# PSUM reads that may run on either of two engines, and a new table for the order of the work: complex-decay linear attention with a token-mixing stage, fp32, one core

## The chip, the cores and the metric

The kernel runs on one core of a Trainium2 chip. The metric is the device time of one execution in microseconds (us). The profile comes from one execution, recorded by the hardware profiler.

## The reference

Two stages follow each other. The first is a linear attention with a complex decay: for each batch (4) and head (8) a 48x48 complex state is decayed and updated in each of 768 steps. The second gates the result by a phase, mixes it over tokens, and adds a channel product:

```python
mag = np.sqrt(a_re * a_re + a_im * a_im)
scale = np.minimum(mag, 0.999) / (mag + 1e-06)
a_re_n, a_im_n = (a_re * scale, a_im * scale)
for t in range(S):
    new_re = ar * S_re - ai * S_im
    new_im = ar * S_im + ai * S_re
    kv = np.einsum('bhd,bhe->bhde', k[:, :, t], v[:, :, t])
    S_re, S_im = (new_re + kv, new_im)
    y[:, :, t] = np.einsum('bhd,bhde->bhe', q[:, :, t], S_re)
...
theta = x @ w_theta                       # x: y as [batch, token, 384]
zr = x * np.cos(theta)
zi = x * np.sin(theta)
y = np.einsum('ts,bsd->btd', w_tok_r, zr) + np.einsum('ts,bsd->btd', w_tok_i, zi)
u = x + y
return (u + np.maximum(u @ w_ch, 0.0)).astype(np.float32)
```

The attention's inputs are fp32. The four weights are float64.

## The kernel before, in words

**Tiling.** The 768 tokens of a batch are cut into six chunks of 128, so there are 24 chunks `n`, each a tile of 128 tokens by 384 = 8 heads x 48. For each chunk `front_a` (L596) takes logarithms of the decay, and TensorE sums them along the tokens with a triangular matrix (`tric`); `front_p` (L674) does the same for the phase (`triq`; the last row of the chunk before comes in through `sel`), rounds it to whole turns by adding a large constant (into `cssn`), and takes sine and cosine. `back` (L713) multiplies `k` and `q` by decay and phase (tiles `hw`), turns them (`kT`, `qT`), forms the masked scores, the chunk's output `x` and the next state. The first four chunks do this in fp32 with TensorE transposes (`old`); later ones split each value into two fp16 halves and turn them by DMA. `theta` (L946) forms the phase of the second stage and `z`, the sine and cosine parts of `x`; `moe_part` and `moe` (L982, L991) mix them over the tokens with `w_tok_r` and `w_tok_i` and add the channel product. The weights arrive as float64, are put together from their bits by three VectorE instructions into a PSUM bank, and are then split into two fp16 halves (`w_load`, `w_split`; the first half is made by `scaled`, L530).

**What sets the order.** The functions above don't issue anything. Each call is recorded as an operation of a `Plan` (L273 on), with the engines that it may run on; `either` (L290) records one that has a form for each of several engines. `order` (L350) then reads a table, `PLACES` (L119), which holds for each step the number of an operation and which of its engines runs it. A negative number stands for a filler, a matmul of constants whose result nobody reads; it goes into a PSUM buffer that is free at that step and is left out where none is free. `emit` (L381) issues the work in the order of the table, so each engine runs its operations in that order. In the profile every operation has line L396, a filler L388, a load of ScalarE's function table L392.

```python
if place < 0:
    kind = next((x for x in PSUM if room.get(x)), None)
...
op = self.ops[place >> 2]
op.engine, op.load = op.engines[place & 3], None
```

**Buffers.** SBUF is divided into pools of equal buffers by size: A (384 fp32 a partition, 48 of them), B (768), C and H for turned tiles, D for scores, E and V for small ones. PSUM has four banks (`bank`; one is kept for scores) and two double banks (`pair`). The names in the rows are these pools, not the variables.

**What may run where, before.** Reading PSUM, `scaled` and `absolute` (L540) use ScalarE only. So do the rounding of the phase in `front_p` and in `theta`, the copies of `kT` and `qT` in the first four chunks, the eviction of `x`, that of `acc` in `moe_part`, and the final Relu in `moe`. Other operations had a choice before: many products between ScalarE, VectorE and POOL.

Of the kernel before, what the change touches and what calls it, by code (L numbers as in the profile page):

```python
# [29 lines left out]
SV = 1.0  # L30
# [101 lines left out]
|RaI3}QQO=Gzaeah8`6fn;ok^s1UEt(KU4*_BRYI1w!PXQcE}xO+qxayuB+H>YA3uA*@$k$HsTwJjU=4hNWrO%G@OC6a6{Ep<#cUTOZ7Ybk5qO{zpXY_)Zc@@vq$elb>SThD
Pqy%9Gr&>a1oBfzfzarGF*YHa1E}*4Y&!n;5OWWyKoOqZ}i~-%<d%Mh??6O!u(EhJGGtO&TMD5bKCjt!gg`Hv|Zk=Y)93<R{ur!8?~?#Q;*=7PTmoB{5u_0V5g_AZfA4}U0n
BPIIW&<FSeK4t8D-VVF-p{1g>qPFb3mrMx9mn^#gr<yRqHeZf&=>JKNpu-gbX`usz%!ZI8EuI|Mw`7Y{-^C1VK~>Hk9qZufLKbxYmUIk3FCpw8<i+tclWuBdCPnN4={FE9zu
wkeo~xlIO+s~hU%&g5jQXJHPO(3CErE*$VMzbU{XEWtADhXZgB4#8nK0t=hsrnD(<{%>7J9fi9p|7Kt_xLMNGHtU;>&Cq6eGqM@ojBUm@o13l8_GV(Uulo;p2A6dceP^?~+1
u=IcGX$kKktHjZCyq8jc%Z;>XMt8-JveK+f#{qgU#XQXcO9l_h$O3zH~6&oNVTH^Sg!J>1J`av|HY->{fScyY=11ZgaP<9;jQpL-j~KR!`LJ-Olc8v%5Q0&(yu$xq80Y-yQ4
@cNglVdbGPzGkbG*0WaYdJl+M=pc+z7c40N51`m_EKC;kDd&nNThwlNJUmV!?7Mq|ZvJ>5j?VxH&BWu7dXv?n&Xo8xMCai(CBATcsrip73n(1zQ2UDkYfBPG}o!I$b2e{g>7
srwsLQSbjbxNZ%I`(F}kOtNu8hH=dLN%BM*PvV27QRJjNDZZ-HH?PUa2j4CXhaRMmD)+~WOlMUX-!6x)#NmJO+i!Clr&{cMN`$(G<8iw)6}#yZ4J3aZP8oI7Q4l5rMEI${Fb
nl-O6o=Ti<B9y8KpQtGHF#8tG_t31ig$)7Y`JRo<#>&2)3!LbuedbigjS3+-07YFqFwvRmJ3Y&EygU2K=wt7EyH)>eC~v(?qG>Ym2GH`fRDcud|}>8B?GCSv$5yUXqJyTY!x
EA7g={@uVXju1$2H?-T=3^YScc$Y-FTh)VKU=lXcj5QO@R5R1m4k*OA_e+e}{l`7jNFzNpW{m9C52Cw`g9b+KQoC~vz02&zcH_H=-Q;fkc%i|KiR08RVO(k=`_cW_etf@)CH  # L140
9m1sr~eRW<R^1+t2SS_P)Je*e~vv_RIT~{m_1OzqViBUunP{U`N=)^s58XC}WNN=6-9xy&v9Zkpz~+I{O^b-EUz$@+&N|7u}2P#rG0>$-UHGdM~q=-}$fI>|So~ci0b)e~&>
sDNH~LJNdohPHCsSBb>F&ZLE0!9EwO`ud-9!sqKvR>O14T#?EAKx;NXK?=^Q?JBz*Lo*zqN@D8#wK!(T&Y43D)x;wp{)gG`9?*Bpc*WLfz?e9SQgPi~t#EN_Wy(=Ly;zt5V5
D6h+B!Wbd7!pSkND@gQX(WSWk>L)!Kic{B-VB)|3uKH;kQ_2QSt2W>v{&A%>{a(_d-c7>UULuG&m*bh^s#>D&pUrTY3;T5I(yx{-d=xius7TTwCFyzkMDz8NDFHbEvm(|xR%
# [313 lines left out]
def fast_path(ctx, tc, gst, q, k, v, a_re, a_im, w_theta, w_tok_r, w_tok_i, w_ch, out):  # L457
# [72 lines left out]
    def scaled(o, i, m, n=DM):  # L530
# [834 lines left out]
```

## Time and profile before

| | before |
|---|---|
| time, median of 3 runs | 415.62 us (413.92 to 416.1) |
| the profiled execution | 416.11 us |
| its span, first to last instruction | 414.4 us |
| mean granted TensorE clock | 0.987 |
| busy: TensorE, VectorE, ScalarE, POOL | 379.7, 366.3, 366.3, 237.6 us |
| fillers | 2 |

The engines are PE (TensorE), PEld (its weight loads), DVE (VectorE), ACT (ScalarE), POOL (GpSimd) and SP (which issues most DMAs). A row of a timeline gives the start, the time of the group, engine, line, operation, output <- inputs, their sizes, how many instructions (x2), and in brackets the engine's idle time just before and what ended it. Drawn times of successive instructions overlap; the distance between two starts tells how fast they follow each other.

### The profile page before, as it was taken

The page shows a single profiled execution, that of the slowest core. Times are in us where ns is not written, and L with a number is a line of the kernel's source. Part 1 is how long each engine was busy: PE and PEld are TensorE (multiplying, and loading weights), DVE is VectorE, ACT ScalarE, POOL GpSimd, SP SyncE. Part 2 cuts the span into 40 slices and gives each one's busy share as a digit, 9 for nine tenths or more (in the row PEclk, how much of TensorE's full clock was granted, in tenths as well). Part 3 has the DMA queues.
Part 4 walks back from the last instruction along what each step waited for, and adds up shares of the span by engine and source line. Part 5 has one row for each costly group of instructions (what it writes and reads, how often), then busy time and mean ns, then how long its engine had stood idle before and what let it go on. Part 6 is the DMA issues. An engine that isn't in the chain of part 4 may idle for free. (4 is left out here: it accounts for less than half of the span.)

```text
span 414.4 us, 9851 instructions
## 1 busy us (share of the span) xinstructions
PE 379.7 (92%) x3431; PEld 262.7 (63%) x3431; DVE 366.3 (88%) x820; ACT 366.3 (88%) x784; POOL 237.6 (57%) x282
## 2 busy tenths in 40 slices
PE   0789999989999999999899999988999999999994
PEld 0268786656676667777566676665667766566662
DVE  5977799989999999999999989899999998785675
ACT  6988999989999898999899999998889895685985
POOL 1054854496789889587646565686677778210000
PEclk9999999699999999999999999999999999999998
DMA  7888882686979898898975899969999999999994
GB/s 231 292 276 289 286 269 89 213 219 168 183 163 206 128 213 191 189 176 206 232 156 107 177 228 174 223 167 216 215 234 183 176 176 257 224 316 354 306 346 157
DMA packets 162934, 89.23 MB, mean 215 GB/s; under 512 B 119360, under 2 KB 161344, under 8 KB 162880
## 3 DMA queue, kind: packets, MB, share of 16 engines
q1 hardware_dynamic: 162880, 88.55, 87.4%
q8 instruction: 28, 0.46, 0.4%
q14 instruction: 26, 0.21, 0.2%
HBM read 55.05 MB, written 4.72 MB: 144 GB/s over the span
## 5 line engine op out<-in xcount | busy, mean ns | idle before, releaser
L396 PE MATMUL bank<-B,B 128*128 128x384 f16 x864 | 170.8, 326 | 0.1
L396 POOL TENSOR_TENSOR A<-A,A 128x384 f16<-128x384 f32 (+2 forms) x86 | 86.6, 1017 | 45.9 <-DMA A<-in_k_dram 21.6
L396 PEld LDWEIGHTS <-B 128*128 128x128 f16 x864 | 79.6, 98 | 47.3 <-issue 6.0
L396 PEld LDWEIGHTS <-C 96*128 96x128 f16 x888 | 64.2, 102 | 20.2 <-issue 5.3
L396 PE MATMUL bank<-C,C 96*128 96x128 f16 (+1 forms) x544 | 59.0, 231 | 5.9 <-ACT D L396 2.0
L396 PE MATMUL bank<-A,D 128*128 128x48 f32 (+1 forms) x448 | 58.6, 232 | 1.2 <-issue 0.7
L396 POOL TENSOR_SCALAR A<-A 128x384 f16<-128x384 f32 (+1 forms) x64 | 41.1, 643 | 32.3 <-ACT A L396 10.5
L392 ACT ACT_TABLE_LOAD x45 | 57.7, 1283 | 0.7
L396 PEld LDWEIGHTS <-A 128*128 128x128 f16 x432 | 39.4, 98 | 25.0 <-DMA A<-A 4.2
L396 ACT ACTIVATE A<-A 128x384 f32<-128x384 f32 (+2 forms) x106 | 52.7, 516 | 2.6 <-DMA A<-in_a_re_dram 2.4
L396 PE MATMUL pair<-A,A 128*128 128x384 f16 x216 | 49.5, 325 | 2.5 <-DMA A<-A 1.1
L396 PE MATMUL bank<-A,C 96*128 96x48 f16 (+1 forms) x456 | 47.3, 194 | 0.0
L396 ACT ACTIVATE B<-B 128x384 f32<-128x384 f32 (+1 forms) x81 | 45.4, 573 | 1.4 <-DMA B<-in_a_re_dram 0.7
L396 DVE SCALAR_TENSOR_TENSOR A<-bank,A 128x384 f32<-128x384 f32 (+1 forms) x69 | 37.6, 551 | 9.6 <-PE bank L396 6.2
L396 PE MATMUL bank<-A,A 128*128 128x384 f16 x216 | 44.3, 325 | 0.7 <-DMA A<-A 0.5
L396 ACT ACTIVATE A<-bank 128x384 f32<-128x384 f32 (+1 forms) x81 | 37.3, 487 | 6.7 <-PE bank L396 5.4
L396 PEld LDWEIGHTS bank<-A,D 128*128 128x128 f32 x256 | 38.6, 190 | 4.2 <-POOL D L396 1.0
L396 POOL TENSOR_TENSOR B<-A,B 128x768 f32<-128x768 f32 x18 | 33.0, 1833 | 9.8 <-ACT B L396 6.6
L396 POOL TENSOR_SCALAR_AFFINE_SELECT D<-D 128x512 f32<-128x512 f32 x32 | 22.6, 706 | 27.7 <-ACT D L396 22.1
L396 ACT ACTIVATE pair<-pair 128x384 f32<-128x384 f32 x72 | 34.6, 480 | 2.7 <-DVE pair L396 1.8
L396 DVE SCALAR_TENSOR_TENSOR A<-A,A 128x384 f32<-128x384 f32 (+2 forms) x59 | 35.5, 610 | 0.3 <-ACT A L396 0.2
L396 DVE SCALAR_TENSOR_TENSOR bank<-B,bank 128x384 int32<-128x384 int32 x60 | 33.1, 558 | 1.2
(142 smaller groups left out, 751.9 us busy)
## 6 DMA issues: line engine op xcount, KB each, us to landing
B<-in_moe_w_tok_r_dram SPq DMA_DIRECT2D x24, 384.0 KB
B<-in_moe_w_tok_i_dram SPq DMA_DIRECT2D x24, 384.0 KB
A<-in_a_re_dram SPq DMA_DIRECT2D x24, 192.0 KB
A<-in_a_im_dram SPq DMA_DIRECT2D x24, 192.0 KB
A<-in_v_dram SPq DMA_DIRECT2D x24, 192.0 KB
A<-in_k_dram SPq DMA_DIRECT2D x24, 192.0 KB
A<-in_q_dram SPq DMA_DIRECT2D x24, 192.0 KB
out_dram<-A SPq DMA_DIRECT2D x24, 192.0 KB
```

The source lines that it names most:

```text
L392: nc.scalar.preload_act_table_set(op.load)
L396: getattr(getattr(nc, op.engine), name)(*[val(x) for x in op.a], **{k: val(x) for k, x in kw.items()})
```

## The change

Seven places get a second engine: `scaled` and `absolute` on PSUM, the two roundings, the `kT`/`qT` copies, `acc`, `x` and the final Relu may each run on ScalarE or on VectorE. A new helper `moved` records such a copy. Computation and matmuls are the same. The table `PLACES` is another one: it sets the order, the engines and the fillers, of which 14 are built instead of 2 (the table has 15 marks; at one no buffer is free). In all 113 operations run on another engine than before. Of the new freedom the table uses, from ScalarE to VectorE, five Relus, four roundings `pn`, three roundings `cssn`, five weight scalings, one `kT` and one `qT` copy, six splittings (`shl`, `z`) and one absolute value; no `x` and no `acc` moves. The other moves are among engines that were allowed before. One output store is issued by POOL instead of SP.

```diff
 PLACES = """
-c-jrt;cLQ<f$;Iz#x}OmMjPAM#x}OGjcsgW8{62%8r#^$Hn#4;dvM^u0|y>BaNxj!0}mW{;DG}N4jede4-OnS@W6o&_`)AJaNxj!0}tGT0}p(_f%o8n$DaKO-&fyH2#5f|H3
...
+c-k#@VQ2!4f#sNt$(W30G-EO*V;qw)8Iv&?lQ9{SF&UFF8Iv)whkLkS!37I0*u#Pa3l=O`u;79P3ocl&U=IrxEV$r;3;wWR!37HzEVy6~3of`|!985?_^urH{=WC%{d$iF03
...
         if i.root.kind in PSUM:
-            ways = (("scalar", "mul", ca(n, True), ways[0][3]),)
-            return pl.either(*ways)
+            return pl.either(("scalar", "mul", ca(n, True), ways[0][3]), ways[2][:2] + (cv(n),) + ways[2][3:])
...
         if i.root.kind in PSUM:
-            return ac.activation(out=o, in_=i, func=AF.Abs, c=AP_)
+            return pl.either(("scalar", "activation", AP_, dict(out=o, in_=i, func=AF.Abs)),
+                             ("vector", "tensor_scalar", C1, dict(out=o.bitcast(I32), in0=i.bitcast(I32), scalar1=ABS_BITS,
+                                                                  scalar2=None, op0=ALU.bitwise_and)))
...
+    def moved(o, i, n, m=None, add=None):
+        pl.either(("scalar", "activation", ca(n, True), dict(out=o, in_=i, func=AF.Identity, **({} if m is None else dict(scale=m)),
+                                                             **({} if add is None else dict(bias=add)))),
+                  ("vector", "tensor_scalar", cv(n), dict(out=o, in0=i, scalar1=m or 1.0, scalar2=None, op0=ALU.mult) if add is None
+                   else dict(out=o, in0=i, scalar1=add, scalar2=None, op0=ALU.add)))
...
-        ac.activation(out=cs, in_=v3(ph[:, :DM]), func=AF.Identity, bias=MAGIC * SPH, c=AP_)
+        moved(cs, v3(ph[:, :DM]), DM, add=MAGIC * SPH)
...
-                    ac.copy(out=hT[nm].of(g)[:R, 4 * g:4 * g + 4].rearrange("r h t -> r (h t)"), in_=tp[:R], c=ca(512, True))
+                    moved(hT[nm].of(g)[:R, 4 * g:4 * g + 4].rearrange("r h t -> r (h t)"), tp[:R], 512)
...
-        ac.activation(out=rn, in_=th[:, :DM], func=AF.Identity, bias=MAGIC * SP, c=AP_)
+        moved(rn, th[:, :DM], DM, add=MAGIC * SP)
...
-        ac.activation(out=cp[:, :DM], in_=cp[:, :DM], func=AF.Relu, scale=1.0 / SP, c=AP_)
+        pl.either(("scalar", "activation", AP_, dict(out=cp[:, :DM], in_=cp[:, :DM], func=AF.Relu, scale=1.0 / SP)),
+                  ("vector", "tensor_scalar", C1, dict(out=cp[:, :DM], in0=cp[:, :DM], scalar1=0.0, scalar2=1.0 / SP,
+                                                       op0=ALU.max, op1=ALU.mult)))
```

TensorE at the start of the program, before. `tric` and `triq` are the scans of the first two chunks, `sel` the row carried into the second; the 96x48 matmuls form the first state out of the tile `hw` (B_179), those with `ident` are its transposes.

```order
L396 MATMUL bank_232<-A_127,tric 128x384
L396 MATMUL bank_231<-A_123,tric 128x384
L396 MATMUL bank_232<-A_129,triq 128x384
L396 MATMUL bank_233<-A_131,triq 128x384
L396 MATMUL bank_233<-A_150,sel 128x384
L396 MATMUL bank_232<-A_134,B_179 96x48
L396 MATMUL bank_230<-ident,B_179 96x128 x4
L396 MATMUL bank_232<-A_134,B_179 96x48 x7
```

The same place now, after the four scans; the second piece follows two transposes later:

```order
L397 MATMUL bank_233<-A_153,sel 128x384
L389 LDWEIGHTS tri_108
L389 MATMUL bank_232<-ones,tri_108 128x256
L389 LDWEIGHTS tri_108
L389 MATMUL bank_232<-ones,tri_108 128x256
...
L397 MATMUL bank_230<-ident,B_179 96x128 x2
L389 LDWEIGHTS tri_108
L389 MATMUL bank_233<-ones,tri_108 128x256
L397 MATMUL bank_232<-A_141,B_179 96x48 x5
```

Five fillers stand between `sel` and the first transposes, and two more among the transposes and state matmuls.

VectorE at the start, before, ahead of the product that makes the first `hw` (B_179, the last row). `A<-A,A` with one operation are products and squares for chunks 2 and 3; the rows on `B_17x` put weights together.

```order
L396 SCALAR_TENSOR_TENSOR A_127<-A_127,bank_231 128x384
L396 TENSOR_TENSOR A_132<-A_132,A_130 128x384
L396 SCALAR_TENSOR_TENSOR A_138<-bank_233,A_138 128x384
L396 TENSOR_TENSOR A_130<-A_132 128x384
L396 TENSOR_TENSOR A_133<-A_133,A_137 128x384
L396 TENSOR_SCALAR bank_233<-B_172 128x384
...
L396 TENSOR_TENSOR A_137<-A_133 128x384
L396 SCALAR_TENSOR_TENSOR A_150<-B_176,bank_232 128x384
...
L396 TENSOR_TENSOR B_179<-A_136,B_176 128x768
```

The same now:

```order
L397 SCALAR_TENSOR_TENSOR A_123<-A_123,bank_231 128x384
L397 SCALAR_TENSOR_TENSOR bank_233<-B_171,bank_233 128x384
L397 TENSOR_SCALAR A_138<-bank_233 128x384
L397 SCALAR_TENSOR_TENSOR A_138<-bank_233,A_138 128x384
L397 TENSOR_SCALAR bank_233<-B_173 128x384
...
L397 TENSOR_TENSOR A_132<-A_147,A_132 128x384
L397 SCALAR_TENSOR_TENSOR A_153<-B_178,bank_232 128x384
L397 TENSOR_SCALAR B_178<-A_153 128x8x48
...
L397 TENSOR_TENSOR B_179<-A_132,B_178 128x768
```

The two products and two squares are gone (three to POOL, one square to ScalarE), and `A_138<-bank_233`, the scaling of a block of `w_theta`, has come.

ScalarE in a stretch that the profile shows at 37 to 48 us, before. `C` are turned `q` and `k` tiles, `bank<-A` and `A<-pair` belong to decay and phase, `B<-B` and `B<-A` to the phase.

```order
L396 COPY C_202<-bank_230 96x512
L396 ACTIVATE B_195<-bank_233 128x384
L396 ACTIVATE A_130,g_xsum<-bank_232 128x384
L396 COPY C_200<-bank_230 96x512
L392 ACT_TABLE_LOAD
L396 ACTIVATE B_188<-A_144 128x8x48
L396 ACTIVATE D_210<-bank_230 128x512
L396 ACTIVATE B_188<-B_188 128x8x48
L392 ACT_TABLE_LOAD
L396 ACTIVATE bank_233<-A_166 128x384
L396 ACTIVATE B_196<-bank_231 128x384
L396 COPY C_202<-bank_230 96x512
```

The same now:

```order
L397 ACTIVATE C_202<-bank_230 96x512
L397 ACTIVATE B_192<-bank_231 128x384
L397 ACTIVATE A_139,g_xsum<-bank_232 128x384
L393 ACT_TABLE_LOAD
L397 ACTIVATE B_190<-A_128 128x8x48 x2
L397 ACTIVATE D_210<-bank_230 128x512
L397 ACTIVATE B_190<-B_190 128x8x48
L393 ACT_TABLE_LOAD
L397 ACTIVATE bank_231<-A_170 128x384
L397 ACTIVATE A_153<-A_151 128x384
L397 ACTIVATE A_140<-pair_234 128x384
```

The two copies that followed the first (`C_200` and again `C_202`) have left ScalarE for VectorE, an absolute value (one of the two `B_190<-A_128`) has come, and the copies that stay are ACTIVATE instead of COPY.

## Rows read from the trace of the kernel before

**Rows 1.** The page's busy time: us (share of the span) and instructions.

```profile
PE 379.7 (92%) x3431; PEld 262.7 (63%) x3431; DVE 366.3 (88%) x820; ACT 366.3 (88%) x784; POOL 237.6 (57%) x282
```

**Rows 2.** Windows by stage: us, then PE, PEld, DVE, ACT, POOL, PEclk, DMA, GB/s.

```profile
0.00:24.00 24.00, 10.40 (x28) 5.67 (x28) 18.78 (x46) 19.42 (x37) 2.06 (x20) 1.00 0.83 270
24.00:40.00 16.00, 14.62 (x77) 11.70 (x77) 11.32 (x22) 13.05 (x29) 10.25 (x10) 1.00 0.80 271
40.00:100.00 60.00, 56.27 (x412) 41.62 (x411) 54.98 (x122) 57.68 (x120) 38.42 (x44) 0.94 0.71 212
100.00:340.00 240.00, 230.93 (x2324) 160.34 (x2323) 228.12 (x489) 222.68 (x461) 173.18 (x192) 1.00 0.90 188
```

**Rows 3.** The chain that ended last, its longest piece: start us, us, what.

```profile
378.71 25.18 PE bank L396 x160
```

**Rows 4.** Timeline of TensorE, 12 to 46 us.

```profile
12.64 2.93 PE L396 MATMUL bank<-A,tric 128*128 128x384 f32 x4 [12.64 <-DMA B<-in_moe_w_tok_r_dram]
...
21.10 0.55 PE L396 MATMUL bank<-A,B 128*96 128x48 f32 x2 [0.55 <-DVE B L396]
...
26.19 2.08 PE L396 MATMUL bank<-C,C 96*128 96x128 f32 x8 [0.50 <-ACT E L396]
28.06 1.49 PE L396 MATMUL bank<-A,tric 128*128 128x384 f32 x2
...
33.23 1.91 PE L396 MATMUL bank<-C,C 96*128 96x128 f32 x8
...
39.16 1.10 PE L396 MATMUL bank<-C,C 96*128 96x128 f32 x8
...
45.24 0.81 PE L396 MATMUL bank<-A,tric 128*128 128x384 f32 x2
```

**Rows 5.** Timeline of VectorE at 16 to 17 us.

```profile
16.56 0.55 DVE L396 TENSOR_SCALAR bank<-B 128x384 int32<-128x384 int32 x1
17.02 0.55 DVE L396 SCALAR_TENSOR_TENSOR A<-bank,A 128x384 f16<-128x384 f32 x1
```

**Rows 6.** Timeline of POOL, its first instruction of the work.

```profile
24.25 1.95 POOL L396 TENSOR_TENSOR A<-A,A 128x384 f32<-128x384 f32 x2 [21.55 <-DMA A<-in_k_dram]
```

**Rows 7.** Timeline of ScalarE, 20 to 36 us.

```profile
20.59 0.49 ACT L396 ACTIVATE B<-bank 128x384 f32<-128x384 f32 x1 [0.54 <-PE bank L396]
20.98 0.48 ACT L396 ACTIVATE A<-bank 128x384 f16<-128x384 f32 x1
...
28.30 0.60 ACT L396 ACTIVATE D<-bank 128x512 f32<-128x512 f32 x1 [0.85 <-PE bank L396]
...
30.43 0.58 ACT L396 COPY C<-bank 96x512 f32<-96x512 f32 x1 [0.36 <-PE bank L396]
...
32.20 0.58 ACT L396 COPY C<-bank 96x512 f32<-96x512 f32 x1 [0.38 <-PE bank L396]
...
35.18 0.60 ACT L396 ACTIVATE D<-bank 128x512 f32<-128x512 f32 x1 [0.82 <-PE bank L396]
```

**Rows 8.** Windows of 1 us, the first of the slow stretch, columns as in rows 2.

```profile
76.00:77.00 1.00, 1.00 (x9) 1.00 (x7) 0.79 (x2) 0.73 (x2) 1.00 (x1) 0.60 0.83 310
```

**Rows 9.** Timelines of VectorE and ScalarE in that stretch: their waits for TensorE.

```profile
77.26 0.56 DVE L396 SCALAR_TENSOR_TENSOR bank<-bank,A 96x384 f32<-96x384 f32 x1 [0.43 <-PE bank L396]
...
83.26 0.49 ACT L396 ACTIVATE B<-bank 128x384 f32<-128x384 f32 x1 [0.35 <-PE bank L396]
```

**Rows 10.** Groups by line and form, the fillers: busy us, mean ns | idle before.

```profile
L388 PE MATMUL bank<-ones,tri 128*128 128x256 f16 x2 | 0.5, 272 | 0.0
```

**Rows 11.** Timeline of TensorE, 91 to 94 us: two waits.

```profile
91.08 0.91 PE L396 MATMUL bank<-A,tric 128*128 128x384 f32 x2 [0.51 <-DVE E L396]
...
93.45 0.91 PE L396 MATMUL bank<-A,tric 128*128 128x384 f32 x2 [0.78 <-ACT A L396]
```

**Rows 12.** Timelines of POOL and VectorE, 271 to 274 us.

```profile
271.88 1.78 POOL L396 TENSOR_TENSOR A<-A,A 96x384 f16<-96x384 f32 x2
...
272.53 1.56 DVE L396 SCALAR_TENSOR_TENSOR A<-A,A 128x384 f16<-128x384 f32 x1
```

More of the change, by code (lines that the diff above doesn't have):

```diff
@@ new lines @@
+iSZA^-z&U~nzG1_K}v2BJV@4FS49Q<2#St+8NVfdUxNS(_>Zbqx3(kN|KX3A7Y#1rHKH3P=MakOe59qo@J`@H<6Mkq2mCpvVA2#YoWydH}Q`=m298V1XP!?-c+B7%SYM2u7g
+p8nMBvvCZDr->;Pc5%?c#zh9dvCW-+d0W#nRf<OS6D{4R;_~!p%q4?&TAy8H?H_PB^GpqgPo61@PXaXs40!)E|Vg}6rs%!ymU<4EuB}G|LQB)O6#Y(XNI=~oM{*|pMDnM3|Q
+^eO+0HCNVK*diLkRq{`T$8|tBDE%i=`~n^C{P8az!jM_R>3KFg`nWKOJIMix8?^+8`-toT460_j6wM|1_3q+#UIxGxb|;rqGGTmDP)CT5l{pb@J0YcHpq?Y+Hi~72r0sfh$5
+;G)$|6sVc%dkunl}8rU0PYT3kUY#%q*fvNm0tt<efbkx(QRDMeaQS_7f_+I;OdV0I(7k>5~3Bv#i2!ML#k7B+veR@nFz_{;UiT5)5swp?4S0qgbk#=3GnqX5>xHE2z}R^Di?
@@ new lines @@
+x7MNc_By=YSx45<_3k>dhOS|2m5u7guQz(@_!_ZBu2t7->-CM++CQ&h>+LmsT>}a0;ySe^t;_4*TJNtT5WU8%v1`OSxlXOq>&!X|N$SBmw}wH#2LB2Cx2?c>a6Ponu7}sT^~
+gHECai_P2p9$vV01mU9$!zaC)aT(wa%}n!3@|0TVQ%Uvz}egt>@R<U<WL$7uQSc!uCMbw4^p?DhdNPeQIbk29kTCE(-mxEqGJAiEa`QzDaC~Ygw?SYwAmC|5igcK5prw;1ns
+Uqgy#pS|c~*wLI7b%j-R`4-UW~I9wmCkJtaaK3yMyV{iga!5K(x(wo?J5ln9uH#3{1&GKe;a}NFhT!6Fn`TAmgxsEAu<!YT!lFF<S0CP$Zgg_W9fc`Z~DMGZ8QL;)-nO7E+M
+P*4@Rw5v;M8V2tZW9B)2mMefC`IKDpzlM~O-Wf%%F6s^RY`zLa0LQNPzfnvrC*7I0VSeLLm4Qo%tAQ`RZ6;`GNcSEBg&{Uri?2S%D@^4W|TjKhN_y9hw@MXnrtPNMW_Uop^<
@@ new lines @@
+8=`m<`fHC5G>4P{eVfm+Jh76r<>DpZ5&Py<@wd5qgGU}bF+YAffe`PM@9-_#vtS4l!k)fftF#lhfKPdR~Th=NwCDKvxTP(a;R4wOUXNI6zclnZDHtsp=JYz5U*C8&}hNCm49
+6{-qt&6FW^cx$edAxsrk)8MzD$kz9^zrWpr+E54TLOrMt4WJ?PE!}_D1t44{Zh!Ml5Lzl1N)|$_3`FhuRc^?ml2jvzP?0K1MXMMUtKw9=3eaOa9MCaIJBzLS!AcoW1yvzcSQ
+Sx4RWVg?TUMpiVJHN7w}A~o^&?emE54Q3imPJV%+8NhzU_o+xz*TcZnQSq8=Z~rMsK6PG1wSx0NXT{+-mDrTR|Ozfktox+Rmy{TcK@yo7f(0j5j75(~a3iPL)^9Hx?TORZ&$
+^l~v0P|8__h-bS{`?XWJg-O)qFh_0!owkxWtire5fgbi^++Nh}{G_Z~DtTu=pa);TrZP!%}><6lE@3Gs_ZFwUJQ#<~Rz(#N*v=QEjY^31mMr<R#k=RIXq&CuU2F}6_Ra2GIe
@@ L207 @@
+%gKgM*oXM?azRFYm=E{ipTsBOBR{E6`jh!we6pY1C;usYroMt-y|2bs|I6uaev!U^luNScABvKP^3{BGU*xOd6J$}AWLfsh0XZm#<gmQ_{I<2}!@fM9(r4@|>~HzPzKHKTa?
+}^|#eE51(wFk3efSsYkIL~c-zWEl`1vo!-@3~9P=DsD_9gkVKH)3-#rkJoQ-SuyZew!Ekri{kvRsj?a!szw4Y?_|<hI=Qb$nf4&)4@2d_&*JH}?JZuVMWDgug3i{XIG6pMOn
+!i?69K;7|JF{+Tc0&-tVNlt1my`1Ah%3#oJ?*Z
 """
@@ L814, in back @@
         x = tile("x", [P, DM], bufs=2 * NCH)
-        ac.activation(out=x, in_=y[:, :DM], func=AF.Copy, scale=SX / (SV * SS),
-                      accum_out=gst["xsum"].of(C.n)[:, n1], c=AP_ + 0.09)
+        to = gst["xsum"].of(C.n)[:, n1]
+        pl.either(("scalar", "activation", AP_ + 0.09, dict(out=x, in_=y[:, :DM], func=AF.Copy, scale=SX / (SV * SS), accum_out=to)),
+                  ("vector", "tensor_scalar", C1 + 0.08, dict(out=x, in0=y[:, :DM], scalar1=SX / (SV * SS), scalar2=None,
+                                                              op0=ALU.mult, op1=ALU.add, accum_out=to)))
         xs[(b, ci)] = x
@@ L988, in moe_part @@
         accs[(b, c)] = acc = tile("acc", [P, DM], bufs=NCH)
-        ac.mul(out=acc, in_=yp[:, :DM], mul=SX / SP, c=AP_)
+        moved(acc, yp[:, :DM], DM, m=SX / SP)
     def moe(b, c, lo=0):
```

160 lines of the change are left out of this document (73 added, 87 removed).

## The prediction

> **What bounds the kernel now.** I read the busy times first, then the windows by stage, then the timelines of the stages that the change touches, last the chain of waits. Over the whole span three engines are nearly full: TensorE 92%, VectorE and ScalarE 88% each [rows 1]. That average hides stages with different limits, and the windows show which [rows 2]. From 100 to 340 us TensorE is busy 230.93 of 240 us, so it has 9.1 us of idle time there; VectorE has 11.9, ScalarE 17.3. TensorE sets that stage. The chain that ended last runs through it too: one of its pieces is 25.18 us of 160 matmuls without a gap from 378.71 us on [rows 3]. From 40 to 100 us it is ScalarE: 57.68 of 60 us busy, 2.3 us idle, against 5.0 on VectorE and 3.7 on TensorE. Before 40 us nothing is full: each engine waits for another in turn, and TensorE is slow. The reader sees that in its timeline [rows 4]: eight 96x128 products take 2.08 and 1.91 us at 26 and 33 us but 1.10 at 39 us, and two scans by `tric` take 1.49 us at 28 us but 0.81 at 45 us. The granted clock of the window reads 1.00 throughout [rows 2], so that column does not show it; the durations do, and by them TensorE ran at 1.2 GHz still at 33 us and at 2.4 GHz from 39 us on. Ahead of it lay a first matmul at 12.64 us, and then gaps and narrow matmuls.
>
> **The change, part by part.** The sum is made against the profiled execution, 416.11 us; the median of the runs shown is 415.62, so 0.5 is taken off at the end.
>
> (a) *The order at the start.* Ahead of the product that TensorE's first state matmul waits for (0.55 us, [rows 4]), four VectorE instructions leave (three to POOL, one to ScalarE) and one scaling of `w_theta` arrives. VectorE's instructions of this size follow each other every 0.46 us (16.56 to 17.02, [rows 5]), so its queue there is 3 x 0.46 = 1.4 us shorter. POOL takes its three at no cost: it sat idle for 21.55 us up to 24.25 [rows 6], and their chunks' scans come only at 28 us and later. On SP's queue the first `k` load now goes ahead of one of `w_theta`; 0.197 MB at the 270 GB/s of this window [rows 2] is 0.7 us by which that block may come later. Bounds -1.4 and +0.7. Several other waits run beside this queue, so I take -0.4.
>
> (b) *Seven fillers at 20 to 24 us.* Their only use can be that TensorE is fast earlier. If it ran at 2.4 GHz from 26 us on, the two groups of 96x128 products would shrink by 0.98 and 0.81 us, and the scan at 28 us and one more like it by 0.68 each [rows 4]: 3.15 us. The path can't win all of it, since it alternates with ScalarE. What ScalarE waits for TensorE in those groups is 0.85 + 0.36 + 0.38 + 0.82 = 2.41 us [rows 7]. Bounds 0 (the clock does not rise earlier) and -2.4; I take -2.0, near the upper one, because the fillers go into the one place where TensorE waits and four of the shrinking groups stand on the alternating path. Late next would be ScalarE's own work, 13.05 of 16 us [rows 2].
>
> (c) *ScalarE relieved from 40 to 100 us.* Six PSUM reads go from ScalarE to VectorE (three weight scalings, one `cssn` rounding, one `kT` copy, one tiny `ec` copy), and four tiny products leave VectorE for POOL. ScalarE's instructions from PSUM follow each other every 0.39 us (20.59 to 20.98, [rows 7]), so it loses 4 x 0.39, 0.5 for the wider copy and under 0.1 for `ec`, 2.1 us in all. VectorE gains 5 x 0.46 less the tiny ones, 1.9 us, out of 5.0 idle. Bounds -2.1 (all of ScalarE's relief reaches the end) and +1.9 (all of VectorE's load does). ScalarE is the fuller by 2.7 us, and VectorE, late next, has half of its idle time left: I take -1.0.
>
> (d) *The slow stretch at 76 to 83 us.* The granted clock falls there (0.60 in 76 to 77 us) after a run of 48-wide fp32 matmuls [rows 8]. The new order keeps that run nearly word for word, with one filler in it, so I leave it as it is: 0. If it did go, the readers that wait for TensorE there would win 0.43 and 0.35 us [rows 9]: bounds 0 and -0.8.
>
> (e) *The fillers' own time.* Fourteen instead of two, 12 x 0.272 = 3.3 us [rows 10]. The seven at the start stand where TensorE waits 0.55 [rows 4], and five stand ahead of scans that wait 0.51 and 0.78 us [rows 11]. Bounds 0 and 3.3 - 0.55 - 0.51 - 0.78 = +1.4. I take +0.1, the end where the waits cover them.
>
> (f) *After 100 us.* The same matmuls in nearly the same order on an engine that is the limit. Some sixty operations change engine in 100 to 340 us, in both directions; priced by the same spacings VectorE gains 1.9 us of work and ScalarE loses 0.9. Both stay beside TensorE's 230.93. After 340 us VectorE gains 3.2, and one output store goes from SP's queue to POOL's; neither is on the chain's gapless piece [rows 3]. I take 0. Bounds: all of TensorE's 9.1 us of idle time gone, or VectorE's 1.9 in full.
>
> Sum: -0.4 - 2.0 - 1.0 + 0 + 0.1 + 0 = -3.3, so 412.8 us for an execution like the profiled one and **412.3 us** for the median.
>
> **A rule against it.** A VectorE instruction with two SBUF operands took 1.56 us at 272.53 while POOL ran two such instructions from 271.88 on [rows 12]; with a PSUM operand and POOL idle one took 0.55 [rows 5]. The Trainium skill (SBUF — State Buffer, "Who interferes with whom") says that the two engines hold a shared port in turn and that the loser blocks for the whole instruction; the trace agrees with its 1.56. By that rule the three products that (a) gives to POOL could block VectorE as long as they would have run on it, (a) would be 0, and the sum -2.9.
>
> **The rivals.**
>
> *The fillers do not lift the clock* (the change doesn't do what it says). For it: from 21.10 us on TensorE is busy most of the time and was still slow at 33 us [rows 4], so activity there is not all it takes; seven fillers are 1.9 us. Against: they are the first unbroken wide work ahead of the narrow matmuls. Then (b) is 0 and the sum -1.3: 414.3 us. Chance 0.20.
>
> *VectorE becomes the bound* (slower). Its idle time from 40 to 340 us is 5.0 + 11.9 us of 300, and the change puts 1.9 + 1.9 us more on it, each read 0.46 there for 0.39 on ScalarE. It decides from the point where VectorE is the last to be ready for TensorE; then the 3.8 us come on top, and if its early delays also eat (a) to (c): 416.11 + 3.8 - 0.5 = 419.4 us. For it: it already has stages of 94 to 95%. Against: in 40 to 100 us ScalarE is the fuller. Chance 0.15.
>
> *POOL and VectorE block each other.* Eighteen two-operand instructions go from VectorE to POOL, eleven of them after 100 us. The worst row shows 1.56 - 0.55 = 1.0 us lost [rows 5, 12]; a fifth of that for each, 18 x 0.2 = 3.6 us, cancels the gain: 415.9 us. Against: seven of them are tiny, and nine of the kind go from POOL to VectorE. Chance 0.06. The rule of the Trainium skill above (SBUF — State Buffer) describes this mechanism.
>
> *More is won after 100 us.* The order shortens a third of TensorE's 9.1 us of waits: 412.3 - 3.0 = 409.3 us. Nothing in the order shows which. Chance 0.09.
>
> **How the numbers follow.** The forecast keeps 0.50, with a range of its own from 410 to 414.5 us; the prediction is its value. A measurement of this kernel can tell about 0.5%, 2.1 us, from no change: faster is below 413.5, slower above 417.7. Faster gets 0.43 of the forecast, all 0.09 of the last rival and 0.05 of the first: 0.57. Slower gets most of the VectorE rival and little else: 0.15. The same is left with 0.28. All lower ends of the terms at once would give 399.8 us and all upper ones 421.5; the range need not reach there. From 407.5 to 418.0 us it holds the forecast, the first, third and fourth rival and leaves out the VectorE one and a little below, under 0.2.
>
> **What would show it.** Right for (b): the 96x128 products and scans between 25 and 35 us at 1.1 and 0.8 us, and ScalarE's 2.41 us of waits for TensorE there shrunk under 1. Right for (a): the first state matmul earlier than 21.10 by a few tenths. Right for (c): ScalarE under 56 of 60 us in 40 to 100 us with that stage's work done about 1 us sooner. Wrong: products still at 2 us at 33 us (first rival); VectorE above 97% from 100 to 340 us, and TensorE's waits named after VectorE (second); many VectorE instructions with two SBUF operands above 1 us (third); or a slow stretch at 76 to 83 us that is gone or longer, which I left alone in (d).

## The result, and the profile after

The changed kernel took 408.78 us (median of 6 runs, 405.99 to 410.87) beside 415.47 for the kernel before (6 runs): ratio 0.985 (0.980 to 0.989). In a second set it took 409.93 us (12 runs, 405.28 to 413.2) beside 413.29 (25 runs): ratio 0.993 (0.989 to 0.997). So it is faster, by 3 to 7 us or 0.7 to 1.5%; 412.3 was forecast. The runs of one kernel spread over 8 to 10 us, and the profiled executions of the kernel before (416.11 us) and of e2 (416.71) are the slowest of their sets; differences of stages below are therefore taken from several profiles.

The page of the changed kernel, busy time, and its windows by stage, to be read against [rows 1, 2]:

```profile
PE 374.3 (92%) x3443; PEld 259.6 (64%) x3443; DVE 368.9 (91%) x824; ACT 359.8 (89%) x778; POOL 236.0 (58%) x285
```

```profile
0.00:24.00 24.00, 9.45 (x36) 5.02 (x36) 17.89 (x43) 19.79 (x37) 5.80 (x24) 1.00 0.85 276
24.00:40.00 16.00, 14.13 (x97) 11.20 (x95) 13.09 (x26) 13.46 (x31) 9.68 (x11) 0.89 0.87 286
40.00:100.00 60.00, 57.03 (x429) 42.48 (x430) 57.97 (x128) 57.58 (x119) 42.15 (x49) 0.97 0.76 218
100.00:340.00 240.00, 234.19 (x2390) 162.87 (x2388) 230.13 (x499) 223.28 (x465) 170.99 (x195) 1.00 0.93 192
```

TensorE's idle time from 100 to 340 us is 5.8 us, after 9.1; but in a second profile of the same kernel it is 8.3, so one profile is not enough for a stage. From 40 to 100 us ScalarE is as full as before (57.58 of 60) and VectorE has caught up with it (57.97): the moved work did not open a gap, it filled one.

The start, as TensorE saw it (timeline of the changed kernel; [rows 4] answer):

```profile
11.40 2.92 PE L397 MATMUL bank<-A,tric 128*128 128x384 f32 x4 [11.40 <-DVE A L397]
...
18.18 1.16 PE L397 MATMUL bank<-A,sel 128*128 128x384 f32 x2
19.18 0.71 PE L389 MATMUL bank<-ones,tri 128*128 128x256 f16 x5
20.87 0.40 PE L397 MATMUL bank<-ident,B 128*96 128x128 f32 x2 [0.98 <-DVE B L397]
...
25.66 2.08 PE L397 MATMUL bank<-C,C 96*128 96x128 f32 x8 [0.68 <-ACT C L397]
27.53 1.49 PE L397 MATMUL bank<-A,tric 128*128 128x384 f32 x2
28.81 0.71 PE L397 MATMUL bank<-ident,B 128*96 128x128 f32 x4
...
31.78 1.16 PE L397 MATMUL bank<-C,C 96*128 96x128 f32 x8
```

An fp32 matmul has two records in the trace. `sel` takes 1.16 us for its two, where a matmul of this shape takes 1.49 at 1.2 GHz and 0.81 at 2.4 GHz [rows 4]: the clock rose within it, ahead of the first filler. The five fillers fit into 0.71 us and the transposes after them run at 2.4 GHz. Then the granted clock falls for 3.4 us, and it does so a second time at 73 us; here are the first and last windows of both stretches, columns as in [rows 2]:

```profile
25.00:26.00 1.00, 0.34 (x1) 0.34 (x2) 0.87 (x2) 0.98 (x3) 0.00 (x0) 0.80 1.06 392
26.00:27.00 1.00, 1.00 (x6) 1.00 (x6) 0.98 (x3) 0.40 (x1) 0.00 (x0) 0.50 1.03 369
...
29.00:30.00 1.00, 0.52 (x5) 0.25 (x3) 0.86 (x3) 0.95 (x3) 1.00 (x2) 0.99 0.98 321
73.00:74.00 1.00, 1.00 (x11) 1.00 (x10) 0.93 (x3) 0.98 (x4) 1.00 (x1) 0.70 0.94 288
76.00:77.00 1.00, 1.00 (x5) 0.54 (x4) 0.58 (x1) 1.00 (x3) 0.55 (x1) 0.60 0.01 2
```

To see in which stage time was won, each matmul of TensorE was matched with the same operation of the changed kernel's profile, and the difference of the two starts was taken (median over the matmuls that start within ten microseconds; positive is later). Each row is one profile:

| lag behind the changed kernel, us | at 40 | 100 | 210 | 300 | 390 |
|---|---|---|---|---|---|
| before | 2.5 | 4.0 | 3.3 | 7.5 | 8.4 |
| changed, profiled again | 0.9 | 0.6 | 0.9 | 2.5 | 3.0 |
| changed, no fillers (e1) | 2.8 | 1.7 | 1.7 | 4.3 | 4.4 |
| before, with the fillers (e2) | 0.7 | 0.7 | 3.5 | 7.9 | 9.0 |
| changed, then before (e5) | -1.4 | -0.4 | -0.3 | 3.4 | 2.5 |
| before, then changed (e6) | 3.4 | 3.5 | 3.9 | 4.4 | 3.9 |
| changed, more fillers (e8) | -0.8 | -1.5 | -1.4 | -1.4 | -2.3 |
| before, five stores less (e10) | 2.7 | 2.7 | 1.8 | 3.4 | 3.9 |
| changed, 18 late reads back (e11) | -0.9 | 0.2 | -0.7 | 1.6 | 5.8 |
| changed, one scaling back (e12) | -0.7 | -0.6 | -0.6 | 2.6 | 3.2 |
| new order, old engines (e3) | 2.0 | 15.6 | 22.2 | 29.5 | 34.2 |
| old order, new engines (e4) | 0.3 | 3.3 | 4.9 | 9.4 | 19.5 |
| changed, 26 reads back (e7) | 3.0 | 11.7 | 12.5 | 16.0 | 19.8 |

Two stages make the gain: up to 40 us, and from 210 to 300 us. Between 40 and 210 us the lags change by -1.1 to 1.1 us, in both kinds of kernel; the exceptions are e2 and the three kernels that are much slower (e3, e4, e7).

### The profile page after: what moved, and what is told of

The parts are those of the page before. It is cut to its first block, busy times and chain, and to the rows that moved or that the text cites. A ratio compares the mean times of both kernels' runs of the same rounds, so it can differ in the third digit from the quotient of the medians.

```text
span 406.1 us, 9863 instructions
## 1 busy us (share of the span) xinstructions
PE 374.3 (92%) x3443; PEld 259.6 (64%) x3443; DVE 368.9 (91%) x824; ACT 359.8 (89%) x778; POOL 236.0 (58%) x285
## 4 chain that ended last, share of the span: by engine, by line
PE 49%; DVE 8%; ACT 4%; DMA 4%; POOL 4%; issue 1%; SPq 0%; DVEq 0%; ACTq 0%; POOLq 0%
PE bank L397 44%; PE pair L397 5%; POOL A L397 3%; DVE A L397 3%; ACT B L397 2%; DVE bank L397 2%; DMA C<-H 1%; ACT A L397 1%; DMA A<-A 1%; DVE pair L397 1%; DMA V<-A 1%; DVE B L397 1%; DVE H L397 1%; ACT bank L397 1%; DMA A<-in_a_im_dram 1%
## 5 line engine op out<-in xcount | busy, mean ns | idle before, releaser
L397 POOL TENSOR_TENSOR A<-A,A 128x384 f16<-128x384 f32 (+2 forms) x92 | 92.3, 1013 | 36.7 <-ACT A L397 25.7
L397 PE MATMUL bank<-C,C 96*128 96x128 f16 (+1 forms) x544 | 56.8, 229 | 3.1 <-ACT D L397 0.9
L397 ACT ACTIVATE A<-A 128x384 f32<-128x384 f32 (+2 forms) x114 | 56.6, 515 | 2.6 <-DMA A<-in_a_re_dram 2.5
L397 PE MATMUL bank<-A,C 96*128 96x48 f16 (+1 forms) x456 | 49.4, 193 | 0.1
L397 PE MATMUL pair<-A,A 128*128 128x384 f16 x216 | 48.3, 325 | 1.1 <-DMA A<-A 1.1
L397 POOL TENSOR_SCALAR A<-A 128x384 f16<-128x384 f32 (+1 forms) x58 | 33.0, 573 | 25.9 <-ACT A L397 16.4
L397 POOL TENSOR_SCALAR_AFFINE_SELECT D<-D 128x512 f32<-128x512 f32 x32 | 21.7, 677 | 37.2 <-ACT D L397 37.0
L397 POOL TENSOR_TENSOR B<-A,B 128x768 f32<-128x768 f32 x18 | 33.7, 1873 | 11.3 <-ACT B L397 5.3
L397 ACT ACTIVATE D<-bank 128x512 f32<-128x512 f32 (+1 forms) x45 | 26.7, 593 | 7.2 <-DVE bank L397 5.1
```

Source lines behind the costliest of these rows:

```text
L397: getattr(getattr(nc, op.engine), name)(*[val(x) for x in op.a], **{k: val(x) for k, x in kw.items()})
```

## The experiments

**The theory** was that the start's gain comes from the fillers, by TensorE's clock, and the gain after 210 us from order and engines there. The rivals: the order alone makes the start's gain; the later gain only carries the earlier start on; only one of order and engines matters.

### e1: the changed kernel without its fillers

```diff
             if place < 0:
-                kind = next((x for x in PSUM if room.get(x)), None)
...
                 continue
```

> The changed kernel without its fillers, else the same. If the fillers raise TensorE's clock earlier at the start: the 96x128 products at 31 us take about 1.9 us again instead of 1.16, work at 40 us comes 1 to 2 us later than in the changed kernel, and the time is 410 to 412 us. If the earlier start comes from the order alone: 408 to 409 us, and the matmuls at 28 to 33 us are as fast as with fillers. If the fillers at 86 us only cost their own time, that place is 0.5 us shorter.

Measured: 409.44 us, ratio to the kernel before 0.993 (0.990 to 0.998). Its timeline at the start, and windows at the ends of its slow stretch:

```profile
18.58 1.26 PE L392 MATMUL bank<-A,sel 128*128 128x384 f32 x2
21.26 0.40 PE L392 MATMUL bank<-ident,B 128*96 128x128 f32 x2 [1.42 <-DVE B L392]
...
26.68 2.08 PE L392 MATMUL bank<-C,C 96*128 96x128 f32 x8 [0.68 <-ACT C L392]
28.55 1.49 PE L392 MATMUL bank<-A,tric 128*128 128x384 f32 x2
...
33.73 1.92 PE L392 MATMUL bank<-C,C 96*128 96x128 f32 x8
```

```profile
22.00:23.00 1.00, 0.81 (x11) 0.69 (x9) 0.89 (x2) 1.00 (x4) 0.00 (x0) 0.90 1.02 352
...
36.00:37.00 1.00, 1.00 (x7) 0.74 (x6) 0.83 (x2) 1.00 (x4) 0.65 (x2) 0.78 0.89 292
```

Here too the clock rose within `sel` (1.26 us) and the transposes at 21.26 us are fast, without any filler. What the fillers change is how long it lasts. Without them TensorE is back at 1.2 GHz from 22.8 to 36.4 us; with them from 25.6 to 29.0, in the second profile from 26.9 to 33.7, in those of e5, e8, e11 and e12 not at all before 70 us. So the fillers hold the clock. Whether they also raise it is open: by the records described below it rose ahead of the first filler in the first profile of the changed kernel and in e2, 0.1 to 1.4 us after it in five others, and without fillers at the start before 20 us in two of five. The lag at 40 us is 2.8 us, that of the old start (2.5, 2.7 and 3.4 in before, e10 and e6): the fillers make the start's gain in the profiles, the order none.

The traces also record when the granted clock changes, and by these records the lag follows how long TensorE ran at 1.2 GHz before 40 us: 19.6 to 21.2 us in e5, e8, e11 and e12 (lag -1.4 to -0.7), 22.2 in the changed kernel (0), 23.0 in e4 (0.3), 23.6 in e2 (0.7), 26.9 in the changed kernel again (0.9), 33.0 in e1 (2.8) and 35.2 to 36.3 in before, e10 and e6 (2.5 to 3.4). Only e3 and e7 do not fit, whose engines stall near 40 us. e4, below, has no filler at the start and yet gets the gain: its clock rose at 16.2 us, fell at 23.0 and was back at 29.9. Why the clock rose before 20 us in e1 and e4, and only after 35 us in before, e10 and e6, no run shows.

The total did not show it: 0.993 here and 0.993 for the changed kernel, each known to about 0.4%, so a gain of 1 to 2 us at the end by the fillers is neither shown nor excluded by the times.

### e2: the kernel before with the fillers

```diff
+MARKS = {44: 5, 60: 1, 62: 1, 566: 1, 802: 4, 815: 1}
...
             out.append(op)
+            for _ in range(MARKS.get(op.n, 0)):
...
+                    op.engine, op.slot = None, self.space[kind][room[kind][0]]
+                    out.append(op)
```

> The kernel before with the same thirteen fillers put at the same matmuls, its order and engines unchanged. If the fillers make the start's gain: work at 40 us comes 1 to 2 us sooner than in the kernel before and the time is 413 to 414 us; if they also shorten the slow stretch at 76 us, 411 to 412. If the order makes it: 415 to 417 us, the matmuls at 26 to 33 us still at 1.9 to 2.1 us.

Measured: 414.42 us, ratio 1.006 (1.003 to 1.010): slower than the kernel before, clear of noise. The start came as the theory said: it leads the kernel before by 1.8 us at 40 us and by 3.3 at 100. Its clock, too, was up ahead of the first filler (a scan in 0.91 us at 17.57):

```profile
17.57 0.91 PE L403 MATMUL bank<-A,triq 128*128 128x384 f32 x2 [0.49 <-DVE A L403]
...
19.25 0.71 PE L395 MATMUL bank<-ones,tri 128*128 128x256 f16 x5
...
201.72 1.46 PE L403 MATMUL pair<-A,A 128*128 128x384 f16 x4 [2.63 <-DMA A<-A]
```

```profile
200.00:204.00 4.00, 2.29 (x9) 1.12 (x10) 0.73 (x4) 0.81 (x2) 1.58 (x2) 0.64 1.15 258
```

All of that lead is gone at 210 us. TensorE waited 0.8 us at 191.8 and 2.6 us at 201.7 us, both times for an `x` tile that is turned by DMA, and its granted clock fell there (0.64 from 200 to 204 us). The tile of the second wait stood 1.6 us in the list of SP, which issues the turns (0.8 in the kernel before), and its matmul started 4.1 us after the end of the issue (2.9 before). So time won early was lost at turned tiles and by the clock; how much each took, and why the kernel ends slower than without fillers, was not tested.

### e3 and e4: order and engines crossed

The order comes from one kernel's table (`PLACES`), the engine of each operation from the other's (`OTHER`); e4 has the two tables the other way round.

```diff
+        engine = {p >> 2: p & 3 for p in np.frombuffer(zlib.decompress(base64.b85decode("".join(OTHER.split()))), np.int16) if p >= 0}
...
-            op.engine, op.load = op.engines[place & 3], None
+            op.engine, op.load = op.engines[engine[place >> 2]], None
```

> The changed kernel's order and fillers, but every operation on the engine of the kernel before. If the freedom of engines makes the gain after 220 us (about 4 us there): 412 to 415 us. If the order alone makes it: 408 to 410 us. Over 417 us would say that the order fits only the engines that it was searched with.

> The order of the kernel before with its two fillers, every operation on the engine of the changed kernel. If the engines make the gain after 220 us: 411 to 413 us. If the order makes it: 415 to 416 us. Over 417 us would say that the engines fit only the order that they were searched with, and that VectorE is late with the added 6 us of work.

Measured: 447.15 us (ratio 1.087, 1.080 to 1.094) and 430.61 us (1.045, 1.037 to 1.052). Crossed as they are, neither half of the change gains anything. My reading is that an order is written for its engines: each runs its list in sequence, and an operation put on another engine takes a place in that engine's list at which its inputs are not ready. In e3 ScalarE stands 3.40 us at 41.66 us before the scaling of a weight block that VectorE has still to assemble, and TensorE then waits 2.63 us for ScalarE.

### e7, e12 and e11: the new freedom undone, whole and in parts

```diff
-            op.engine, op.load = op.engines[place & 3], None
+            op.engine, op.load = "scalar" if op.n in NEW else op.engines[place & 3], None
```

> The changed kernel with the 26 PSUM reads of the new freedom back on ScalarE, everything else (order, fillers, the other 87 moves) as changed. If the new freedom carries the gain after 220 us: 3 to 5 us slower than the changed kernel. If it carries only the relief of ScalarE in 40 to 100 us: 1 to 2 us slower. If the other moves and the order make the gain: within 1 us of it. Much over 5 us would say that the order is tied to each of its engines, as the two crossed kernels showed.

Measured: 426.42 us (1.033, 1.028 to 1.038). Its lag behind the changed kernel grows by 10 us between 30 and 50 us. Four rows of its timelines, the first two of ScalarE:

```profile
33.36 0.85 ACT L398 ACTIVATE B<-bank 128x384 f16<-128x384 f32 x2
...
42.92 0.49 ACT L398 ACTIVATE B<-bank 128x384 f16<-128x384 f32 x1 [3.22 <-DVE bank L398]
...
46.20 0.66 PE L398 MATMUL bank<-ident,B 128*96 128x128 f32 x2 [3.03 <-ACT D L398]
...
50.07 0.56 DVE L398 SCALAR_TENSOR_TENSOR A<-bank,A 128x384 f32<-128x384 f32 x1 [5.60 <-ACT bank L398]
```

ScalarE stands for 3.22 us before the scaling of a weight block that VectorE has still to assemble; the scores behind it in ScalarE's list keep TensorE waiting 3.03 us, and VectorE then waits 5.60 for ScalarE. The granted clock is at half besides, 0.51 from 46 to 56.4 us. I took one scaling to be the cause, and e12 puts back operation 396 alone:

> The changed kernel with one instruction back on ScalarE: the scaling of a block of w_tok_i near 37 us (operation 396). If that instruction, waiting in ScalarE's queue for VectorE's assembly of the block, is what stalls the kernel with all 26 back: 5 to 9 us lost at about 40 us and a time of 413 to 418 us. If it takes several to stall it: under 1 us lost.

Measured: 410.12 us (0.993, 0.989 to 0.996), as the changed kernel. But this does not test the row. By the order of ScalarE's list the scaling that stands at 42.92 us in e7 is operation 427, the next block of `w_tok_i`; operation 396 is the first of the two at 33.36 us and waits for nothing. So e12 shows that 396 alone costs nothing. Whether 427 alone makes the stall, or it takes several, was not tried. e11 puts back the 18 that run after 100 us:

> The changed kernel with only those 18 of the 26 PSUM reads back on ScalarE that run after 100 us. If they carry the gain after 220 us: as the changed kernel up to 170 us, then 3 to 9 us lost (the kernel with all 26 back lost 9 us after 100 us). If the 9 us were the aftermath of that kernel's early stall: within 1 us of the changed kernel.

Measured: 415.4 us (1.008, 1.005 to 1.011), 1.5% above the changed kernel by the two ratios. It is level with it at 210 us (-0.7) and 5.8 us behind at 390, where the changed kernel's second profile is 3.0 behind. From 160 us on TensorE's waits are these, first with the 18 back, then of the changed kernel (us in total, times, longest):

```profile
PE bank L398 <- DVE A L398: 4.2, 8, 1.0
PE bank L398 <- ACT A L398: 2.5, 3, 1.7
...
PE bank L398 <- POOL H L398: 1.0, 1, 1.0
```

```profile
PE bank L397 <- DVE A L397: 1.3, 2, 0.8
PE pair L397 <- DMA A<-A: 1.1, 1, 1.1
PE bank L397 <- ACT D L397: 0.9, 1, 0.9
```

That is an upper bound for the freedom's worth, since the order was not searched again for the 18. But its sign is clear: VectorE with less work makes TensorE wait for VectorE longer, because what VectorE needs comes later from a fuller ScalarE. VectorE's own longest waits for ScalarE in the same stretch say so, first two rows with the 18 back, then the longest of the changed kernel:

```profile
DVE B L398 <- ACT B L398: 7.1, 5, 3.4
DVE A L398 <- ACT bank L398: 5.7, 6, 1.8
```

```profile
DVE pair L397 <- ACT pair L397: 1.6, 3, 0.7
```

### e6 and e5: the two kernels spliced at 210 us

```diff
+        first, then = (np.frombuffer(zlib.decompress(base64.b85decode("".join(t.split()))), np.int16) for t in (PLACES, OTHER))
+        cut = list(first >> 2).index(2293) + 1
+        done = set(first[:cut] >> 2)
...
+        for place in [*first[:cut], *rest]:
```

> The order and engines of the kernel before up to the score matmuls at 210 us (operation 2293), from there those of the changed kernel. If the gain after 220 us is made by the order and engines there: 3 to 4 us faster than the kernel before. If it needs the earlier start: the time of the kernel before, within 1 us.

> The converse of the last splice: order and engines of the changed kernel up to operation 2293 at about 207 us, from there those of the kernel before. If the gain after 220 us is made there by order and engines: the lead of 3 to 4 us at 200 us stays, nothing is added after, the end 2 to 4 us later than the changed kernel's, 411 to 413 us. If it comes from the earlier start: as fast as the changed kernel, within 1 us.

Measured: e6 411.31 us (0.994, 0.990 to 0.998), e5 411.77 us (0.998, 0.993 to 1.002). From 210 to 300 us the three profiles with the old second half (before, e2, e5) lose 4.2, 4.4 and 3.7 us against the changed kernel; those with the new one (changed again, e1, e6, e8, e12) lose 1.6, 2.6, 0.5, 0.0 and 3.2. The means are 4.1 and 1.6. So the later gain, some 2.5 us, is made there and does not need the early start: e6 has none and keeps it. The two groups nearly meet (3.7 in e5, 3.2 in e12), and e1's 2.6 holds a fall of the clock at 275 to 279 us. The times agree for e6, 0.6% faster than the kernel before and clear of noise; e5, with the new first half alone, is not clear of it.

### e10: fewer stores in the kernel before

What TensorE waits for there differs in the kernel before and the changed one (205 to 300 us; the kernel before first):

```profile
PE bank L396 <- ACT D L396: 1.2, 2, 1.0
PE bank L396 <- DVE D L396: 1.2, 2, 1.0
PE pair L396 <- DMA A<-A: 1.1, 3, 0.5
PE bank L396 <- DMA C<-H: 0.7, 1, 0.7
```

```profile
PE bank L397 <- DVE A L397: 1.3, 2, 0.8
PE bank L397 <- ACT D L397: 0.9, 1, 0.9
PE bank L397 <- ACT A L397: 0.2, 1, 0.2
```

The waits for DMA, which fetch turned tiles, are gone in this profile. Over all profiles they are a part of the difference: between the matmuls that the changed kernel runs at 210 and 300 us TensorE stands 4.9, 5.1 and 4.4 us in before, e2 and e5, of that 1.9, 3.1 and 0.6 for DMA; with the new order (changed, again, e1, e6, e8, e12) it stands 1.7, 3.1, 2.7, 2.4, 1.6 and 3.9 us, of that 0, 1.0, 0.8, 0.4, 0.6 and 2.0 for DMA. In the means that is 2.3 us less, 1.1 of it for DMA; the rest is less waiting for VectorE and ScalarE. SP issues those turns, and its list at 217 to 230 us in the kernel before has hardly a gap (the second column is how long SP spends on one issue):

```profile
217.36 0.66 SPq L396 DMA_DIRECT2D V<-A  x1
218.39 3.91 SPq L396 DMA_TRANSPOSE C<-H  x1
222.41 0.52 SPq L396 DMA_DIRECT2D A<-in_a_im_dram  x1
223.04 1.22 SPq L396 DMA_TRANSPOSE A<-A  x1
...
227.83 1.73 SPq L396 DMA_TRANSPOSE C<-H  x1
229.66 1.05 SPq L396 DMA_DIRECT2D V<-A  x1
230.80 0.39 SPq L396 DMA_DIRECT2D out_dram<-A  x1
```

The `kT` tile turned at 227.83 was ready at 220.2, so it waited 7.7 us for its place in SP's list; in the changed kernel 5.3. Five more tiles between 223 and 252 us that waited 1.4 to 2.1 us wait 0.0 to 1.3 there. To test it, e10 takes five stores out of that list in the kernel before (part of the output stays unwritten):

```diff
         for op in out:
+            if getattr(op, "n", None) in SKIP:
+                continue
```

> The kernel before without the five output stores that SP issues between 231 and 279 us (it leaves that part of the output unwritten); it takes 2 us of issue time and 1 MB out of SP's queue. If TensorE's waits for turned tiles at 220 to 290 us come from SP's queue: these waits shrink by 1 to 2 us and work at 300 us comes 1 to 2 us sooner than in the kernel before, counted from 210 us. If they come from late producers or from the DMA engines alone: no change above 0.5 us there.

Measured: 411.81 us (1.000, 0.995 to 1.004). In its profile the stage from 210 to 300 us loses 1.6 us instead of about 4.1, the level of the new order, and TensorE's waits for `A<-A` are gone; the time as a whole doesn't show it. That SP's list is what held the turned tiles is therefore supported by one profile and not proved by the times; e5, which has the old list after 210 us, waits only 0.6 us for DMA there.

### e8: more fillers, and the changed kernel again beside it

```diff
+MARKS = {106: 8, 65: 4, 585: 2, 589: 2, 597: 2}
```

> The changed kernel as it is, beside the next three, since the time of the kernel before differed by 2.5 us between two sets of runs. Every theory expects the first set's distance to the kernel before: 6 to 7 us, or 4 if a part of that was the spread of the runs.

> The changed kernel with 18 more fillers: twelve where TensorE waits 1.19 and 0.68 us at 22 to 26 us, six inside the run of 48-wide matmuls at 70 to 73 us. If such runs and waits are what lowers the clock: no slow stretch at 26 to 29 us nor at 74 to 77 us, work at 100 us 1.5 to 2.5 us sooner, the time 406 to 408 us or 1 to 2 us below the changed kernel. If what is won early is given back to the DMA queue: the milestones at 100 us as said, the end unchanged. If the fillers only cost their time: 0.5 to 1 us slower.

Measured: 409.93 us for the changed kernel as it is (0.993, 0.989 to 0.997) and 408.47 us with 18 more fillers (0.990, 0.986 to 0.995). Neither slow stretch is in its profile (granted clock 1.00 in both windows):

```profile
24.00:34.00 10.00, 8.66 (x58) 6.30 (x58) 8.39 (x18) 9.06 (x22) 6.06 (x6) 1.00 0.85 282
73.00:78.00 5.00, 4.47 (x26) 2.71 (x25) 4.84 (x11) 4.71 (x10) 2.99 (x5) 1.00 0.43 116
```

Work at 100 us comes 1.5 and 2.1 us sooner than in the changed kernel's two profiles, as expected, and the lead lasts to the end; the profiled execution, 405.52 us, is the fastest of the eight. One profile does not show that the 18 did it: e5, e11 and e12, with the changed kernel's fillers alone, have no slow stretch before 70 us either and the same lag at 40 us, and e1, with none, has no second one. The 1.5 us over the changed kernel are less than the two intervals can separate.

## Why the prediction was right, step by step

The direction was right, and 408.78 and 409.93 us lie in the range of 407.5 to 418.0, though just below the forecast's own range of 410 to 414.5. The main term, the fillers, is there at 40 us in the profiles. At the end no time shows it: e1 without fillers is as fast as the changed kernel in its second set (0.993), e5 with the new first half is at 0.998, and e2 with fillers is slower. What the times do show is the stage after 210 us (e6, 0.994), which the prediction put at nothing. That the sum came out in the range is therefore in part luck.

**(a) The order at the start**, forecast -0.4: nothing. The first scan came 1.2 us sooner (11.40 after 12.64), but the first matmul on `hw` without fillers started at 21.26 us, after 21.10 before. VectorE's shorter list just ended in waits of its own for ScalarE (0.42, 0.36 and 0.23 us between 15 and 20 us).

**(b) The fillers**, forecast -2.0: the gain at 40 us is right in kind and too small. Five profiles of the changed start lag by 0, 0.9, -1.4, -0.9 and -0.7 us at 40 us, four without its fillers by 2.5, 2.7, 3.4 and 2.8: the means differ by 3.3 us. The cap of 2.41 us held where it was made: from 26 to 36 us e5, e11 and e12, whose clock did not fall, gain 2.4 to 2.5 us on the kernel before, and ScalarE's waits for TensorE there shrink to 0.8 us in e5 and e12 (2.0 in the first profile of the changed kernel). The other 0.6 to 1.1 us they had won before 26 us, which the step did not count. What it did not see either is that the clock rises without fillers, ahead of them, and can fall again at 26 us, as it did in two of the five. The rival that the fillers do nothing for the clock is out; what is shown is that they hold it. (The eight products and two scans that the prediction reads from [rows 4] are four and one, of two records each; the sum does not change by that.)

**(c) ScalarE relieved**, forecast -1.0: not seen. From 40 to 100 us the lag of the two groups changes by less than their spread of some 1.5 us, so 1.0 is not excluded either. VectorE's 5.0 us of idle time were taken as cover; they were used up (2.0 us left), and ScalarE is as full as before.

**(d) The slow stretch**, forecast unchanged: it stayed, for 3.4 us in both profiles of the changed kernel and 6.8 in e11, after 6.8 in that of the kernel before [rows 8] and 3.4 in e10; in e1 and e8 it is missing. Its length varies between executions, so the change gets no credit for it.

**(e) The fillers' own time**, +0.1: one takes 0.11 us of TensorE where five stand in a row (5 in 0.71 us, drawn 0.27 each), so all fourteen cost 1.5 us and not the 3.8 of the drawn durations. At the place of the five at 86 us e1 waits 0.21, 0.28 and 0.32 us, so these lay in waits; for the others it was not taken apart.

**(f) After 100 us**, forecast 0: this step failed. The prediction took TensorE's list to be the same and its waits to stay. They did not: 210 to 300 us gave about 2.5 us, 1.1 of them by waits for turned tiles and the rest by waits for VectorE and ScalarE. Which of the moves did it stays open. The fourth rival, more won after 100 us at 409.3 us, describes the outcome, and its price was about right; its chance of 0.09 was too low, and I had not read SP's list, where a part of it lay.

**The other rivals.** VectorE is fuller, 230.13 of 240 us, and did not become the bound; e11 takes work off it and is slower. POOL and VectorE do not block each other more: the ten VectorE instructions of the kind that took 1.56 us [rows 12] now take 552 ns in the mean, after 731. The three products given to POOL at the start ran at 11.74 to 14.6 us without a longer instruction on VectorE beside them, so (a) did not come to nothing that way. Every VectorE instruction there read or wrote PSUM and read at most one operand from SBUF, so the port rule of the Trainium skill (SBUF — State Buffer, "Who interferes with whom"), which is about two operands in SBUF, was not put to the test.

## What to carry to other kernels

An order written out for in-order queues and the choice of engines belong together: here neither could be exchanged alone, and a moved operation is read by what stands behind it in its new list. Where matmuls start narrow and broken by waits, look at their durations against later ones of the same shape; a few wide matmuls in the waits can hold the clock, but a gain in the first 40 us is not yet one at the end, and the times have to show it. Before calling a stage bound by one engine, read the queue that issues its transfers too, and compare several profiles: here two of the same kernel differed by 3 us at the end. Before undoing one instruction to test a wait, make sure by the order of the list that it is the one that waits.

## What was not expected of the hardware

- In the kernel before the granted clock reads 1.00 over the first 40 us [rows 2] while a scan takes 1.49 us at 28 us and 0.81 at 45 us [rows 4]: the trace's first record of the clock is at 35.2 us, and ahead of it only the durations tell.
- The same kernel differs in its clock from one execution to the next: in its first slow stretch the changed kernel spent 3.4 us in one profile and 6.8 in the other, and e5 and e11, with the same start, had none.
- SP spent 1.2 to 4.1 us on the issue of one DMA transpose in the kernel before, for 0.3 to 0.7 on nearly nine of ten plain transfers. By the sum of issue times its list was full for 15 to 20 of every 20 us from 100 to 340 us.
